# Channel relu on ScalarE and residual addition on GpSimd for three of four batches, in a recurrence-and-mixer kernel

## Chip, cores and metric

The kernel runs on one core of a Trainium2 chip. The metric is device time in microseconds for one execution. The time before is the median of 7 runs, 212.28 us (211.8 to 213.85). The engines are called by their usual names and the profile's: TensorE (PE; PEld is its weight load), VectorE (DVE), ScalarE (ACT), GpSimd (POOL) and SyncE (SP), whose queue issues most transfers.

## What is computed

The first half is a linear recurrence over 768 steps for 4 batches and 8 heads of 40 channels. The second half is a mixer on the result `x` (4 x 768 x 320):

```python
for t in range(S):                      # for every batch and head
    y[:, :, t] = einsum('bhd,bhde->bhe', rt, state)
    Sa = einsum('bhde,bhe->bhd', state, at)
    state = state * wt[:, :, None, :] - einsum('bhd,bhe->bhde', Sa, bt)
    state = state + einsum('bhd,bhe->bhde', vt, kt)
...
theta = x @ w_theta
zr, zi = x * cos(theta), x * sin(theta)
u = x + einsum('ts,bsd->btd', w_tok_r, zr) + einsum('ts,bsd->btd', w_tok_i, zi)
return u + maximum(u @ w_ch, 0.0)
```

The last line is the one that the change touches: the channel matmul `u @ w_ch`, its relu, and the residual addition of `u`.

## The kernel before, in words

The 768 steps of a batch are cut into 6 tiles of 128 steps; the 24 tiles of the 4 batches are worked one behind the other, all 8 heads at once.

For each tile, `prep` takes logarithms and cumulative sums of the decay (`lw`, `ex`, `sx`, `we`), scales the inputs on GpSimd (`kb` L696, `ah` L700, `v` L705) and transposes them on TensorE, ScalarE copying the results out of PSUM (L625). `scores` makes four 128x1024 blocks of step-by-step products on TensorE (L750, matmuls that use 64 rows of the array) and multiplies each by a mask on DVE (L755: `psi`, `phi`, `lamv`, `lamu`). `recurrence` solves the tile and carries the state to the next one: matmuls L783 and L789, copy `nx` on ScalarE (L795), matmuls L801, copy `nu` (L805), matmuls L822, then `sum` on DVE (L833) and the new state `gt` on GpSimd (L837). `readout` makes the tile's `x` (matmuls L885 to L894, then L901 on DVE), and `theta` multiplies it by `w_theta` (L910) and stores it through ScalarE (`th`, L920).

When a batch's tiles are done, `sines` takes sine and cosine on ScalarE (`cs`, L934, with another table of functions than the exponentials: a table load at L934 and one back at L1070), and GpSimd multiplies them by `x` into `zr` and `zi` (L946). Then `mix_row` makes each of the batch's 6 rows: 12 matmuls of 320 columns (L964), `u` on DVE (L974), a transpose of `u` (L865), the channel matmul (L910 with `wch`), the last step `oo` on DVE (L983) and the store (L986, on SP's queue). The rows of one batch run beside the tiles of the next; those of the last batch end the kernel.

The order of the work isn't the order of the code. Every instruction group is entered in a plan with an engine, a cost in nanoseconds, what it reads and writes, and a due time: `TIMES` by tile or row, plus `OFF` by kind, plus `ADJ` by the entry's number. A planner walks through modelled time, picks for each engine the entry with the least due time plus a penalty for waiting (`WAIT`) and for changing ScalarE's table (`TSWITCH`) or TensorE's 64- or 128-row form (`PSWITCH`), and deals out the 8 PSUM banks. What it yields is a fixed program: five queues, each worked in its order. Ahead of 14 us of planned time TensorE's gaps are filled with warm-up matmuls (L1064).

`u` has 4 buffers, `oo` has 3. What the change touches is the last step of `mix_row`:

```python
add("DVE", "oo", q, lambda: nc.vector.scalar_tensor_tensor(
    out=oo, in0=ps(ck)[:, 0:DM], scalar=0.0, in1=u[:, 0:DM], op0=ALU.max,
    op1=ALU.add), 488, [ck, ("u", q % 4)], [("oo", q % 3)], at="row")
add("SP", "st", q, lambda: nc.sync.dma_start(out=out_r[bi, j], in_=oo), 350,
    [("oo", q % 3)], [], at="row", work=550)
```

Of the kernel before, what the change touches and what calls it, by code (L numbers as in the profile page):

```python
# [11 lines left out]
AF = mybir.ActivationFunctionType  # L12
ALU = mybir.AluOpType
# [217 lines left out]
def tail(n):  # L231
# [4 lines left out]
    ah=-52.11, ch=49.75, cs=-52.92, ea=13.09, egd=-104.06, egt=-143.6, ekb=68.26, enu=18.9,  # L236
    enut=-16.67, er=39.64, eth=-122.81, eut=-51.5, ev=51.59, ew=15.76, ewt=-188.11, ex=-112.25,
    exp=-6.71, ext=81.47, gd=18.03, gt=35.48, kb=-27.06, la=-23.53, lb=-26.79, lk=-21.79,
    ln=-12.91, loadr=-13.5, lv=-12.45, lw=-26.87, mlu=184.93, mlv=69.19, mphi=153.16,
    mpsi=133.2, nu=29.59, nut=8.5, nx=-47.05, oo=28.87, r=113.01, row=16.53, sin=118.93,  # L240
    slu=-23.3, slv=25.75, sphi=-42.65, spsi=-87.98, st=17.74, ta=-28.45, th=19.17, tkb=15.03,
    tr=9.43, tv=-9.54, uadd=-2.7, ut=65.67, v=-4.95, wdma=168.22, wgt=-13.67, wi=-19.42,
    wt=-25.32, x0=-70.93, xt=30.93, y=-14.3, z=183.08)
WAIT, TSWITCH, PSWITCH = 1393.81, 654268.0, -24719.0
TIMES = dict(
    tile=[
        -86.14, -69.58, -37.21, -14.07, -14.8, 2.38, 2.2, 20.46, 24.1, 33.31, 50.51, 55.4,
        82.34, 92.68, 113.54, 132.24, 115.95, 137.46, 159.05, 157.81, 174.6, 187.04, 146.21,
        211.1],
    row=[  # L250
        69.81, 38.63, 41.84, 41.57, 7.21, -11.02, 134.23, 117.63, 149.79, 184.39, 169.21,
        207.36, 168.53, 187.12, 225.65, 155.58, 163.42, 84.66, 319.84, 314.41, 401.22, 514.77,
        559.98, 419.59],
    rel=[
        -33.63, 39.77, 64.32, 56.8, -226.72, 86.46, 80.14, -8.42])
ADJ = {
    0: -6.37, 1: 8.3, 2: -7.89, 3: -12.04, 4: -3.57, 5: 1.5, 6: 4.24, 7: 0.99, 8: 6.36,
    9: 16.34, 10: 5.24, 11: -0.26, 12: -20.38, 13: -2.84, 14: -4.42, 15: 1.56, 16: 1.04,
    17: 0.94, 18: -5.49, 19: 25.76, 20: -18.69, 21: 14.82, 22: -35.14, 23: 15.33, 24: 9.3,
    25: -0.9, 26: -5.18, 27: 5.69, 28: -20.76, 29: -7.52, 30: 16.91, 31: -9.14, 32: 26.44,  # L260
    33: -24.48, 34: 0.09, 35: -6.49, 36: -4.07, 37: 19.8, 38: -3.88, 39: 31.9, 40: -21.52,
    41: 27.32, 42: 5.23, 43: 3.89, 44: 2.28, 45: 6.35, 46: -3.55, 47: 4.36, 48: -0.72,
    49: 17.27, 50: 2.89, 51: 1.03, 52: -8.63, 53: 4.26, 54: -15.55, 55: -4.73, 56: -4,
    57: -2.18, 58: -36.01, 59: 3.02, 60: 4.49, 61: 28.68, 62: 0.32, 63: 2.69, 64: 4.61,
    65: 15.52, 66: 3.33, 67: 7.9, 68: 19.92, 69: -24.92, 70: -19.56, 71: 7.32, 72: 2.32,
    73: 21.16, 74: -8.51, 75: 1.62, 76: 1.58, 77: 12.52, 78: 2.22, 79: 1.98, 80: -8.26,
    81: 9.13, 82: 8.74, 83: -3.97, 84: 6.44, 85: 30.89, 86: 20.89, 87: 4.91, 88: -18.97,
    89: -1.02, 90: -39.76, 91: -5.91, 92: 11.36, 93: -22.13, 94: 15.62, 95: 10.71, 96: 3.64,
    97: 16.75, 98: -15.21, 99: -9.38, 100: 13.66, 101: 49.35, 102: 24.08, 103: -4.48,
    104: -8.09, 105: 38.54, 106: 3.08, 107: 28.48, 108: -9.04, 109: 14.05, 110: -12.9,  # L270
    111: -1.07, 112: -11.73, 113: 3.1, 114: -8.22, 115: -12.87, 116: 8.88, 117: -2.6,
    118: -0.69, 119: -6.56, 120: 18.35, 121: -0.64, 122: -22.22, 123: -4.96, 124: 15.3,
    125: 6.35, 126: -27.45, 127: 3.64, 128: 1.51, 129: -6.26, 130: -3.4, 131: -2.3, 132: -1.17,
    133: -13.37, 134: -1.7, 135: -0.01, 136: 16.69, 137: -7.08, 138: -0.5, 139: 18.08, 140: 4,
    141: -0.64, 142: 9.44, 143: -8.52, 144: -11.7, 145: -10.97, 146: 0.84, 147: 21.7, 148: -33,
    149: -4.17, 150: -2.19, 151: -0.74, 152: -4.13, 153: -2.44, 154: 0.36, 155: 21.02,
    156: 8.83, 157: -17.49, 158: -2.38, 159: 37.49, 160: 13.92, 161: 5.6, 162: 7.91,
    163: -2.34, 164: 28.5, 165: -7.61, 166: -16.91, 167: 4.86, 168: -4.3, 169: -16.93,
    170: -8.59, 171: -1.86, 172: -10.98, 173: -29.57, 174: 1.8, 175: 2.06, 176: -1.04,
    177: -55.47, 178: -2.04, 179: -13.59, 180: -0.73, 181: 3.9, 182: -0.75, 183: -1.04,  # L280
    184: 12.94, 185: 2.38, 186: -6.65, 187: 3.87, 188: 3.65, 189: -4.21, 190: 26.25, 191: 1.91,
    192: 0.59, 193: 11.95, 194: 22.42, 195: -5.3, 196: -18.83, 197: -8.08, 198: -3.49,
    199: -3.43, 200: -4.4, 201: -6.72, 202: 12.03, 203: -1.66, 204: -17.55, 205: -31.63,
    206: 15.51, 207: -10.93, 208: -17.43, 209: -4.4, 210: 7.83, 211: -4.44, 212: 13.12,
    213: -41.95, 214: -19.49, 215: 14.31, 216: 13.59, 217: 7.03, 218: 16.79, 219: -9.08,
    220: 4, 221: -6.77, 222: -7.57, 223: 21.01, 224: -7.74, 225: 12.36, 226: 10.83, 227: -6.61,
    228: 9.69, 229: 21.68, 230: 5.78, 231: 18.68, 232: 16.71, 233: -6.88, 234: -3.19,
    235: 13.7, 236: -11.83, 237: 1.49, 238: -4.5, 239: -1.11, 240: -0.98, 241: -29.01,
    242: -4.88, 243: -5.11, 244: 5.26, 245: -11.98, 246: 9.82, 247: 29.31, 248: 21.76,
    249: 14.42, 250: 4.41, 251: 56.91, 252: 9.47, 253: 9.53, 254: -11.2, 255: 37.04, 256: 5.9,  # L290
    257: -22.1, 258: -17.04, 259: -17.49, 260: -41.5, 261: -4.34, 262: -3.59, 263: -5.07,
    264: 30.34, 265: 21.1, 266: -20.31, 267: -2.53, 268: 20.04, 269: 24.18, 270: 48.62,
    271: -24.19, 272: 9.87, 273: -6.59, 274: -9.32, 275: -1.27, 276: -0.86, 277: 12.73,
    278: -26.81, 279: 8.18, 280: 28.16, 281: -38.2, 282: 0.14, 283: -1.42, 284: 8.61,
    285: -2.21, 286: -0.27, 287: -1.87, 288: -5.91, 289: 4.5, 290: -1.14, 291: 2.76,
    292: -3.89, 293: 15.58, 294: 0.21, 295: -2.51, 296: -19.83, 297: -21.12, 298: -13.52,
    299: 2.18, 300: -17.63, 301: -12.94, 302: 10.61, 303: -10.77, 304: 11.43, 305: -26.03,
    306: 14.21, 307: 28.47, 308: 11.2, 309: 5.66, 310: -14.04, 311: -10.82, 312: -16.59,
    313: 4.16, 314: -35.35, 315: 16.87, 316: 10.71, 317: -0.13, 318: -19.63, 319: -22.89,
    320: 27.35, 321: -9.39, 322: -2.42, 323: -2.29, 324: -1.41, 325: -19.26, 326: 16.71,  # L300
    327: -20.77, 328: -0.92, 329: -9.88, 330: -10.4, 331: -5.42, 332: -16.26, 333: 20.65,
    334: -7.61, 335: 0.88, 336: -2.65, 337: 25.72, 338: 30.25, 339: 7.19, 340: -17.23,
    341: -7.43, 342: 12.14, 343: -2.56, 344: -0.53, 345: 2.9, 346: -3.34, 347: 0.67,
    348: -0.46, 349: -15.55, 350: 29.58, 351: 12.01, 352: -0.77, 353: 7.51, 354: 22.83,
    355: 16.14, 356: 23.38, 357: -23.33, 358: -8.15, 359: 0.72, 360: -17.66, 361: 13.97,
    362: -12.12, 363: -15.15, 364: 30.36, 365: 36.88, 366: 6.29, 367: -27.99, 368: 9.94,
    369: -2, 370: -14.99, 371: -18.91, 372: 12.8, 373: 19.03, 374: 12.92, 375: -3.65,
    376: 5.67, 377: 19.41, 378: 16.41, 379: 17.22, 380: 0.63, 381: 13.8, 382: 20.91,
    383: 24.19, 384: 20.15, 385: -1.66, 386: -5.07, 387: -10.46, 388: -29.92, 389: 16.74,
    390: -9.91, 391: 16.93, 392: 1.46, 393: 20.84, 394: -5.9, 395: -0.31, 396: 2.31,  # L310
    397: -37.32, 398: -8.5, 399: -15.55, 400: 0.56, 401: 1.35, 402: 3.17, 403: -25.65,
    404: 11.11, 405: 11.05, 406: 2.98, 407: -3.53, 408: 15.93, 409: 4.06, 410: 7.86,
    411: -7.48, 412: 10.14, 413: 5.27, 414: -27.1, 415: 18.16, 416: 18.6, 417: -34.62, 418: 17,
    419: -22.51, 420: 42.85, 421: 20.44, 422: 33.09, 423: 3.62, 424: -7.25, 425: 7.78,
    426: 36.81, 427: -3.15, 428: -13.12, 429: -33.79, 430: -9.03, 431: 1.34, 432: -23.24,
    433: -17.08, 434: -6.39, 435: -1.15, 436: 8.79, 437: 14.46, 438: 30.49, 439: -4.36,
    440: -4.34, 441: 2.29, 442: 25.14, 443: 26.81, 444: -8.67, 445: -14.52, 446: 14.84,
    447: 27.71, 448: -14.26, 449: 6.26, 450: 12.09, 451: 16.34, 452: -8.66, 453: -1.78,
    454: 28.27, 455: -6.98, 456: -2.29, 457: 46.71, 458: -19.59, 459: -12.28, 460: 34.9,
    461: -2.98, 462: 3.94, 463: -23.98, 464: 3.42, 465: 30.57, 466: 1.45, 467: 5.05,  # L320
# [153 lines left out]
def kernel(  # L474
# [14 lines left out]
    nc = tc.nc  # L489
# [3 lines left out]
    DM = H * D  # L493
# [608 lines left out]
```

## Time and profile before

| what | us |
|---|---|
| median of 7 runs (lowest, highest) | 212.28 (211.8, 213.85) |
| the profiled execution | 212.28 |
| its span, first to last instruction | 210.5 |
| TensorE busy | 195.4 |
| DVE busy | 174.2 |
| ScalarE busy | 154.4 |
| GpSimd busy | 127.4 |
| mask multiplies L755, 96 of them | 116.6 |
| row matmuls L964, 288 of them | 81.3 |
| last steps L983, 24 of them | 11.3 |

TensorE ran at its full granted clock throughout. Matmuls overlap each other, so the sum of their durations is more than the time that TensorE needs for them: the 288 row matmuls take 0.30 us each, but start 0.136 us apart where nothing holds them up. Busy times of the other engines overlap a little as well: an instruction of 0.48 us on DVE is followed by the next one's start 0.40 us after its own.

A line of the profile's groups reads: line, engine, operation, output and input by the program's names, shapes, count, then busy time in us, mean ns of one, and idle time of the engine ahead of it with what ended it. A line of the stretches reads: from:to, length, busy us (instructions) of PE, PEld, DVE, ACT and POOL, granted clock, share of the DMA engines, GB/s. A line of the waits reads: who waited for whom, us in total, how many times, the longest.

### The profile page before, as it was taken

Reading aid. Unit: us, or ns where it says so; the run is one execution under the profiler, and the core shown is the slowest. Engines: PE = TensorE matmul, PEld = TensorE weight load, DVE = VectorE, ACT = ScalarE, POOL = GpSimd, SP = SyncE. Lnnn points to the kernel's source line nnn. Section 1 sums busy time; section 2 is a strip of 40 time slices with the busy share of each in tenths; the row PEclk is TensorE's granted clock in tenths of the full one; section 3 lists DMA queues with packets and bytes.
Section 4 is the critical chain, followed back from the end, with each engine's and each line's share of the span. In section 5 each row is a group of like instructions: output and inputs, shape, how many; then the busy total and the mean of one; then the engine's idle time right before and its main releaser. Section 6 shows DMA issues by size and latency. Waiting matters only on the chain.

```text
span 210.5 us, 8135 instructions
## 1 busy us (share of the span) xinstructions
PE 195.4 (93%) x3375; PEld 157.2 (75%) x3375; DVE 174.2 (83%) x277; ACT 154.4 (73%) x366; POOL 127.4 (61%) x186
## 2 busy tenths in 40 slices
PE   7777988788999999999999999999999999999993
PEld 7655876677878788887777888778887777887771
DVE  7399986799999987998788778989999987657533
ACT  2685878998799869945997967978799978371211
POOL 3206266779978987875098773786558964614000
PEclk9999999999999999999999999999999999999999
DMA  6999989989999998989989989999994010003122
GB/s 113 203 167 214 168 156 183 181 167 170 194 197 156 204 163 162 159 155 193 194 163 197 191 148 164 176 155 215 202 192 100 0 69 3 31 22 107 39 89 93
DMA packets 134181, 30.82 MB, mean 146 GB/s; under 512 B 125824, under 2 KB 134144, under 8 KB 134144
## 3 DMA queue, kind: packets, MB, share of 16 engines
q1 hardware_dynamic: 131712, 27.54, 67.1%
q0 software_dynamic: 2432, 2.77, 8.5%
q8 instruction: 26, 0.43, 0.8%
q14 instruction: 11, 0.09, 0.1%
HBM read 29.13 MB, written 3.93 MB: 157 GB/s over the span
## 4 chain that ended last, share of the span: by engine, by line
PE 58%; ACT 9%; DVE 5%; POOL 3%; issue 2%; POOLq 0%; ACTq 0%; DVEq 0%
PE ps_s L964 16%; PE ps_s L622 10%; PE ps_s L910 8%; PE ps_d L750 7%; PE ps_s L865 3%; ACT L934 2%; PE ps_s L801 2%; PE ps_s L894 2%; ACT cs L934 2%; PE ps_s L892 1%; PE ps_s L1012 1%; PE ps_s L789 1%; PE ps_s L885 1%; PE ps_s L733 1%; PE ps_s L783 1%
## 5 line engine op out<-in xcount | busy, mean ns | idle before, releaser
L696 POOL TENSOR_TENSOR kb<-raw_kb,ex 128x320 bf16<-128x320 f32 x44 | 37.7, 869 | 23.4 <-ACT vT L625 9.7
L964 PE MATMUL ps_s<-zr,wtok_r 128*128 128x320 bf16 x144 | 40.7, 299 | 0.0
L964 PE MATMUL ps_s<-zi,wtok_i 128*128 128x320 bf16 x144 | 40.6, 299 | 0.0
L755 DVE TENSOR_TENSOR psi<-ps_d,mask_p 128x1024 bf16<-128x1024 f32 x24 | 29.2, 1217 | 3.7 <-PE ps_d L750 3.7
L755 DVE TENSOR_TENSOR lamu<-ps_d,mask_p 128x1024 bf16<-128x1024 f32 x24 | 29.2, 1216 | 2.2 <-PE ps_d L750 2.1
L755 DVE TENSOR_TENSOR phi<-ps_d,mask_n 128x1024 bf16<-128x1024 f32 x24 | 29.1, 1214 | 1.3 <-PE ps_d L750 1.1
L755 DVE TENSOR_TENSOR lamv<-ps_d,mask_p 128x1024 bf16<-128x1024 f32 x24 | 29.1, 1213 | 0.4 <-PE ps_d L750 0.3
L946 POOL TENSOR_TENSOR zr<-cs,x 128x320 bf16<-128x320 f32 x23 | 17.9, 795 | 14.1 <-ACT cs L934 14.0
L700 POOL TENSOR_TENSOR ah<-raw_a,we 128x320 bf16<-128x320 f32 x22 | 19.0, 865 | 6.6 <-ACT we L689 3.5
L974 DVE TENSOR_TENSOR u<-ps_s,x 128x320 bf16<-128x320 f32 x24 | 11.6, 487 | 10.7 <-PE ps_s L964 10.7
L946 POOL TENSOR_TENSOR zi<-cs,x 128x320 bf16<-128x320 f32 x23 | 18.0, 797 | 1.3 <-ACT cs L934 1.3
L625 ACT COPY kbT<-ps_s 128x512 f32<-128x512 f32 x24 | 14.2, 592 | 5.7 <-PE ps_s L622 5.3
L750 PE MATMUL ps_d<-aT,kbT 64*128 64x128 bf16 x384 | 17.2, 218 | 0.9 <-ACT aT L625 0.4
L964 PEld LDWEIGHTS <-wtok_r 128*128 128x128 bf16 x144 | 14.1, 98 | 4.2
L625 ACT COPY uT<-ps_s 128x192 f32<-128x192 f32 x24 | 7.5, 320 | 12.8 <-PE ps_s L865 12.5
L964 PEld LDWEIGHTS <-wtok_i 128*128 128x128 bf16 x144 | 14.1, 98 | 3.8
L622 PE MATMUL ps_s<-ident,kb 128*128 128x128 bf16 x192 | 14.9, 219 | 1.1 <-POOL kb L696 0.6
L685 DVE TENSOR_TENSOR sx<-ps_s,lw 128x320 f32<-128x320 f32 x24 | 11.5, 483 | 5.1 <-ACT ex L682 5.1
L892 PE MATMUL ps_s<-kb,lamv 128*128 128x40 bf16 x192 | 15.3, 180 | 0.1
L894 PE MATMUL ps_s<-kb,lamu 128*128 128x40 bf16 x192 | 14.9, 179 | 0.4 <-DVE lamu L755 0.4
L983 DVE SCALAR_TENSOR_TENSOR oo<-ps_s,u 128x320 f32<-128x320 f32 x24 | 11.3, 484 | 4.4 <-PE ps_s L910 4.3
L750 PEld LDWEIGHTS <-kbT 64*128 64x128 bf16 x384 | 11.2, 94 | 4.8 <-issue 1.5
(119 smaller groups left out, 583.7 us busy)
## 6 DMA issues: line engine op xcount, KB each, us to landing
raw_a<-in_a_dram SPq DMA_DIRECT2D x24, 160.0 KB, 4.3
raw_kb<-in_b_dram SPq DMA_DIRECT2D x24, 160.0 KB, 3.9
raw_w<-in_w_dram SPq DMA_DIRECT2D x24, 160.0 KB, 4.2
raw_v<-in_v_dram SPq DMA_DIRECT2D x24, 160.0 KB, 4.2
raw_kb<-in_k_dram SPq DMA_DIRECT2D x24, 160.0 KB, 3.7
raw_r<-in_r_dram SPq DMA_DIRECT2D x24, 160.0 KB, 3.8
out_dram<-oo SPq DMA_DIRECT2D x24, 160.0 KB, 1.9
wrow_r<-in_moe_w_tok_r_dram POOLq DMA_DIRECT2D x6, 192.0 KB, 5.1
```

What stands on the lines that cost most here:

```text
L622: nc.tensor.transpose(out=dst[:, c:c + 128], in_=pair(src, g), identity=ident)
L625: nc.scalar.copy(out=out.bitcast(FP32), in_=in_)
L696: lambda j=j: (nc.vector if fast else nc.gpsimd).tensor_tensor(out=paired(kb[:, j])[:, :, :, 0:D], in0=natural(raw_kb[s4][:, j]), in1=invW ...
L700: lambda: (nc.vector if fast else nc.gpsimd).tensor_tensor(out=paired(ah)[:, :, :, 0:D], in0=natural(raw_a[i % 6]), in1=Wi, op=ALU.mult),
L750: nc.tensor.matmul(t[:, q, g, :], lhsT=lhs[rows(q), g * 128:(g + 1) * 128], rhs=rhs[rows(q), g * 128:(g + 1) * 128], start=True, stop=True)
L755: add("DVE", kindm, i, lambda: nc.vector.tensor_tensor(out=dst.rearrange("p a b c -> p (a b) c"), in0=ps(p).rearrange("p a (g c) -> p (a g ...
L892: nc.tensor.matmul(o, lhsT=lamv[:, p, g, :], rhs=kb[:, 0, h, 0:D], start=first, stop=False, skip_group_check=True)
L894: nc.tensor.matmul(o, lhsT=lamu[:, p, g, :], rhs=kb[:, 1, h, 0:D], start=False, stop=True, skip_group_check=True)
L910: nc.tensor.matmul(dst, lhsT=lhs[:, kt, :], rhs=rhs[:, kt, :], start=kt == 0, stop=kt == 2)
L946: nc.vector if fast else nc.gpsimd).tensor_tensor(
L964: nc.tensor.matmul(ps(pk)[:, 0:DM], lhsT=wtok[nm][:, s, j * 128:(j + 1) * 128], rhs=zs[c][:, s], start=n == 0 and c == 0, stop=n == NT - 1 ...
L974: add("DVE", "uadd", q, lambda: nc.vector.tensor_tensor(out=u[:, 0:DM], in0=ps(pk)[:, 0:DM], in1=x[:, 0:DM], op=ALU.add), 488, [pk, ("x", ...
```

## The change

For the rows of the first three batches (18 of 24) the last step is taken apart: ScalarE writes the relu of the channel matmul from PSUM into `oo`, and GpSimd adds `u` to `oo` in place. For the last batch's 6 rows it stays on DVE. All due times are other ones too, and the entries behind the first row have other numbers, since 18 entries are new; so the planner yields another order on every engine.

```diff
@@ OFF, WAIT, TSWITCH, PSWITCH, TIMES, ADJ: every value is another one
-    ... oo=28.87, r=113.01, row=16.53, ...
-WAIT, TSWITCH, PSWITCH = 1393.81, 654268.0, -24719.0
+    ... oo=-24.03, oop=0.1, r=86.08, relu=62.85, ...
+WAIT, TSWITCH, PSWITCH = 1802.17, 792912.0, -33791.0
@@ mix_row
         oo = oo_t[q % 3]
-        add("DVE", "oo", q, lambda: nc.vector.scalar_tensor_tensor(
-            out=oo, in0=ps(ck)[:, 0:DM], scalar=0.0, in1=u[:, 0:DM], op0=ALU.max,
-            op1=ALU.add), 488, [ck, ("u", q % 4)], [("oo", q % 3)], at="row")
+        if bi < B - 1:
+            add("ACT", "relu", q, lambda: nc.scalar.activation(
+                out=oo, in_=ps(ck)[:, 0:DM], func=AF.Relu), 432, [ck], [("oo", q % 3)], at="row")
+            add("POOL", "oop", q, lambda: nc.gpsimd.tensor_tensor(
+                out=oo, in0=oo, in1=u[:, 0:DM], op=ALU.add), 800,
+                [("oo", q % 3), ("u", q % 4)], [("oo", q % 3)], at="row")
+        else:
+            add("DVE", "oo", q, lambda: nc.vector.scalar_tensor_tensor(
+                out=oo, in0=ps(ck)[:, 0:DM], scalar=0.0, in1=u[:, 0:DM], op0=ALU.max,
+                op1=ALU.add), 488, [ck, ("u", q % 4)], [("oo", q % 3)], at="row")
         add("SP", "st", q, lambda: nc.sync.dma_start(out=out_r[bi, j], in_=oo), 350,
             [("oo", q % 3)], [], at="row", work=550)
```

The lines of `mix_row` behind this place stand some lines lower in the changed kernel: the relu is L987, the addition L989, the step left on DVE L993, the store L996; those ahead of it are 3 lines lower (L755 becomes L758).

## The prediction, made before the result was known

> **What bounds the kernel now.** I read the busy table first, then the chain, then the stretches, then the spacing of TensorE's starts.
>
> ```profile
> span 210.5 us, 8135 instructions
> PE 195.4 (93%) x3375; PEld 157.2 (75%) x3375; DVE 174.2 (83%) x277; ACT 154.4 (73%) x366; POOL 127.4 (61%) x186
> ...
> PE 58%; ACT 9%; DVE 5%; POOL 3%; issue 2%; POOLq 0%; ACTq 0%; DVEq 0%
> ```
>
> PE fills the span and most of the chain, but its busy time counts overlapped matmuls. The busy times by stretch (PE, PEld, DVE, ACT, POOL) say where it is short of work:
>
> ```profile
> 15.00:30.00 15.00, 13.41 (x266) 10.82 (x265) 14.87 (x20) 11.02 (x30) 7.20 (x9) 1.00 1.00 186
> ...
> 45.00:60.00 15.00, 13.68 (x290) 11.32 (x287) 14.47 (x17) 13.20 (x38) 13.94 (x20) 1.00 1.01 175
> 60.00:70.00 10.00, 9.31 (x194) 7.58 (x191) 10.00 (x14) 9.77 (x20) 8.47 (x14) 1.00 1.04 187
> 70.00:131.00 61.00, 60.30 (x1039) 49.02 (x1034) 51.84 (x74) 47.37 (x114) 43.00 (x61) 1.00 0.94 172
> 131.00:170.00 39.00, 38.44 (x755) 31.49 (x755) 37.33 (x49) 34.60 (x83) 29.51 (x42) 1.00 0.73 143
> 170.00:207.20 37.20, 37.07 (x449) 27.42 (x443) 23.56 (x41) 16.86 (x40) 10.66 (x15) 1.00 0.15 53
> ```
>
> Up to 70 us DVE is full and PE is not; from 70 us on, where the first mixing row starts, PE is full. To see how full, I add up issue time from start-to-start spacings in the PE timeline:
>
> ```profile
> 130.29 0.21 PE L789 MATMUL ps_s<-v,psi 128*128 128x40 bf16 x2
> 130.43 0.40 PE L750 MATMUL ps_d<-aT,kbT 64*128 64x128 bf16 x8
> 130.76 0.58 PE L910 MATMUL ps_s<-wch,uT 128*128 128x320 bf16 x3
> 131.18 0.30 PE L964 MATMUL ps_s<-zr,wtok_r 128*128 128x320 bf16 x1
> ```
>
> A 320-column matmul takes 0.136 us of PE, one of 128 columns 0.0555, of 80 columns 0.0355, of 40 or fewer 0.025, a warm-up one 0.107. Eight score matmuls (L750, 64 rows) take 0.225, and each run of them costs 0.19 more for going into and out of the 64-row form (0.11 us instead of 0.025 ahead of the run above, 0.148 behind its last matmul instead of 0.053). With the counts of the groups: 459 x 0.136 + 872 x 0.0555 + 320 x 0.0355 + 888 x 0.025 + 68 x 0.107 + 96 x 0.225 + 67 runs x 0.19 = 186.5 us within rounding. The last matmul ends at 207.2 us, so PE stands idle for 20.7 us. Ahead of the first row matmul (70.1 us) the sum is 55.2: 14.9 us idle. Behind it, 131.3 of 137.1: **only 5.8 us idle, over two thirds of the kernel**. By the semaphore that each of these late gaps waited for, about 1.5 us are DVE's, 0.4 DVE's or ScalarE's, 2.2 ScalarE's. The 3.3 us behind the last matmul (last addition, store, end) stay.
>
> **The change, part by part.** The profiled run took 212.28 us, which is also the median; 1.8 us of it lie outside the span. I sum against it.
>
> *Removed:* 18 of the 24 instructions of L983 on DVE. Each takes 0.48 us busy and moves the next start by 0.40:
>
> ```profile
> 90.41 0.48 DVE L983 SCALAR_TENSOR_TENSOR oo<-ps_s,u 128x320 f32<-128x320 f32 x1
> 90.81 1.21 DVE L755 TENSOR_TENSOR lamv<-ps_d,mask_p 128x1024 bf16<-128x1024 f32 x1
> ```
>
> That is 8.7 us of busy time, 7.2 us of DVE's queue, all behind 78 us, where PE and not DVE is full.
>
> *Added:* 18 ScalarE relus and 18 GpSimd additions. A relu on 128x320 from PSUM isn't in the trace; the nearest rows are the plain copy and the slower exp of nearly the same shape:
>
> ```profile
> L920 ACT COPY th<-ps_s 128x320 f32<-128x320 f32 x23 | 9.8, 427 | 2.7 <-PE ps_s L910 2.4
> L682 ACT ACTIVATE ex<-ps_s 128x328 f32<-128x328 f32 x24 | 10.6, 447 | 3.0 <-PE ps_s L678 2.9
> L946 POOL TENSOR_TENSOR zr<-cs,x 128x320 bf16<-128x320 f32 x23 | 17.9, 795 | 14.1 <-ACT cs L934 14.0
> L696 POOL TENSOR_TENSOR kb<-raw_kb,ex 128x320 bf16<-128x320 f32 x44 | 37.7, 869 | 23.4 <-ACT vT L625 9.7
> ```
>
> I take 0.43 us for a relu (bounds 0.427 and 0.447) and 0.80 for an addition, which is contiguous as zr is (bounds 0.795 and 0.869). Together 7.7 us on ScalarE and 14.4 us on GpSimd, which are 73% and 61% busy. Between 131 and 170 us, where three relus go, ScalarE has 4.4 us free and needs 1.3. Hidden as work; not as a wait (second rival).
>
> The Trainium skill speaks against both halves. "ScalarE: Activation LUTs", section "Rules for kernel authors", wants relu and add on VectorE, which it calls up to about three times faster; the rows here say 0.427 us for a copy out of PSUM on ScalarE against 0.484 for L983 on DVE. By the rule 18 relus would be up to 26 us of ScalarE, an estimate, instead of 7.7. "GPSIMD Engine Reference", section "4.1 Engine selection", calls GpSimd about half as fast for two inputs; L946 agrees in kind, 0.795 us on GpSimd against 0.493 on DVE for the last tile.
>
> *A longer hand-over:* PSUM to output was one instruction, and is now relu, semaphore, addition, some 0.75 us more (0.43 + 0.80 - 0.48). A store waits so much longer in SP's queue with loads of the next tiles behind it; ten of the 18 have loads behind them. The loads run tiles ahead, and behind 60 us no engine waits for a load by more than 1.1 us, so I cost this at nothing; without that cover it is 0.75 us a store.
>
> *Moved:* all due times changed, so every queue has a new order. Its instruction lists show three things. ScalarE loads 11 tables in place of 13 (L934 and L1070, 1.283 us each): 2.6 us back. PE has the same work less two warm-ups, but 74 runs of scores in place of 67: +1.33 - 0.21 = **+1.1 us of PE**, 187.6 in all. And the first row stands earlier: ahead of its first `u` (L974) DVE has 36 mask multiplies (spacing 1.13) in place of 38, 10 `sx` in place of 12, 7 `x` in place of 8: 58.5 us of queue in place of 62.0. PE has 53.9 ahead of the first row matmul in place of 55.2.
>
> **The sum.** Up to the first row DVE sets the pace (10.00 of 10.00 us busy just before it), so that row should come up to 3.5 us sooner. PE's work ahead of it falls by only 1.3, so 2.2 us of PE's 14.9 us of idle time go; none go if ScalarE's sines or the loads pace that stage. I take 2.2, as the DVE column is nearest to full. Behind the first row DVE is relieved and PE can get back at most the 1.9 us that DVE shares in; I take 1.0, since half of such gaps are latency of one step and not a queue (bounds 0 and 1.9). The relus cost ScalarE's queue something: bounds 0 and 1.7 (DVE waited 1.7 us for this very matmul between 60 and 195 us); I take 0.5. Sum: 212.28 + 1.1 - 2.2 - 1.0 + 0.5 = **210.7 us**. The bounds make 209.3 with everything good (212.28 + 1.1 - 2.2 - 1.9), and lower if rows pulled forward also fill other early gaps: 14.9 us lie there, and I allow 1 us, 208.3.
>
> **The rivals.**
> - *DVE's free time stays DVE's.* PE is the bound behind 70 us, and the front is paced by the sines: GpSimd's zr waits 14.0 us for `cs` in 4 waits. Then only +1.1 and -1.0 remain: 212.3 us. For it: 5.8 us idle in 137. Against: the full DVE column.
> - *Slower: ScalarE's queue becomes the wait.* A relu waits for its channel matmul as L983 did, but in a queue with the recurrence behind it: of the 18 relus two have `nx` and one each `nu` and `gd` within two places, and two of GpSimd's additions have a new state (L837) so close behind.
>
> ```profile
> DVE oo L983 <- PE ps_s L910: 4.3, 5, 1.2
> POOL gt L837 <- DVE sum L833: 7.1, 7, 3.7
> ```
>
>   Five waits in 24 of 0.86 us are 3.2 in 18; with two states held up for 0.75 each, 4.7 us at most. If the 1.7 us that fall between 60 and 195 us reach PE and nothing is won, the time is 212.28 + 1.1 + 1.7 = 215.1. It decides from about 1 us of net loss, 213.3, on: I give it 214.2. For it: PE's late gaps are ScalarE's more than DVE's (2.2 against 1.5), so work moves onto the engine that PE waits for. Against: ScalarE is 78% busy between 70 and 131 us, DVE 85%.
> - *Nothing changes in kind:* that L983 still runs for these rows is excluded by the lists: 6 are left on DVE.
>
> **How the numbers follow.** Forecast of 210.7 (208.3 to 211.2): 0.42. Unchanged within 0.5%, which is about what a measurement can tell from no change (211.2 to 213.3): 0.28. Slower (213.3 to some 216): 0.30. Leaving out about a tenth at each end gives 208.3 to 214.8.
>
> **What would show it.** Right: the first row matmul starts 1 to 3.5 us before 70.1; PE's idle time ahead of it falls from 14.9 to about 12.7; DVE is some 8.7 us less busy; relus near 0.43 us, additions near 0.80; from there on PE at 96% or more. Wrong: the first row no earlier (first rival); waits of ScalarE for L910 ahead of relus above 2 us, longer waits of GpSimd ahead of L837 (now L840) and late PE idle time above 6 us (second rival).

## The result, and the profile after

The changed kernel takes 213.27 us (median of 24 runs, 212.05 to 214.59) against 212.20 us (61 runs) of the kernel before. The ratio is **1.0044** (95% interval 1.0029 to 1.0060): slower by 0.93 us by the ratio (1.07 us between the medians). That is clear of no change by the interval, and under 0.5%. The forecast was 210.7 us; the result lies in the case of "unchanged within 0.5%", which had a chance of 0.28. The profiled execution took 213.0 us, 0.7 more than the one of before.

The page of the changed kernel, its span, busy times and chain:

```profile
span 211.2 us, 8126 instructions
...
PE 195.5 (93%) x3373; PEld 157.1 (74%) x3373; DVE 167.3 (79%) x259; ACT 158.2 (75%) x382; POOL 141.1 (67%) x204
...
PE 64%; ACT 14%; DVE 10%; DMA 4%; issue 3%; SPq 1%; POOL 1%; ACTq 0%; DVEq 0%
```

DVE is 6.9 us less busy, GpSimd 13.7 us and ScalarE 3.8 us more: the work moved as written, and the span grew all the same. PE has the same busy time within 0.1 us. The chain now goes through ScalarE for 14% (9% before), DVE for 10% (5%) and transfers for 4%.

The stretches of the changed kernel (PE, PEld, DVE, ACT, POOL busy, then clock, DMA share, GB/s):

```profile
45.00:60.00 15.00, 14.62 (x309) 12.13 (x304) 14.81 (x18) 13.15 (x38) 12.71 (x19) 1.00 0.97 173
60.00:70.00 10.00, 9.58 (x178) 7.59 (x176) 9.86 (x13) 9.64 (x19) 9.31 (x15) 1.00 1.07 184
70.00:131.00 61.00, 60.40 (x1038) 48.82 (x1036) 49.11 (x68) 49.04 (x118) 49.21 (x69) 1.00 0.95 175
131.00:170.00 39.00, 38.03 (x768) 31.29 (x766) 37.19 (x46) 36.19 (x90) 30.76 (x44) 1.00 0.76 149
170.00:208.00 38.00, 37.03 (x441) 27.61 (x440) 20.39 (x33) 16.82 (x44) 16.99 (x23) 1.00 0.14 50
```

Up to 70 us PE is fuller than before (14.62 instead of 13.68 in 45 to 60 us): the front is better. From 70 to 170 us DVE has lost 2.9 us of work and PE has gained nothing from it.

The groups of the new step:

```profile
L989 POOL TENSOR_TENSOR oo<-oo,u 128x320 f32<-128x320 f32 x18 | 14.4, 798 | 13.9 <-ACT oo L987 13.7 <-DMA raw_v<-in_v_dram 0.2
...
L987 ACT ACTIVATE oo<-ps_s 128x320 f32<-128x320 f32 x18 | 7.9, 437 | 5.7 <-DMA out_dram<-oo 3.0 <-PE ps_s L913 2.0 <-POOL zr L949 0.6
```

An addition takes 0.798 us and a relu 0.437 us, as priced. But a relu waited 3.0 us for a transfer, the store that still held its output buffer.

**Where the 0.7 us went.** I add up PE's issue time for both kernels by the spacings of the prediction (done by program on each start, which puts the sums of before at 15.1 and 6.2 us of idle time instead of 14.9 and 5.8):

| us | before | after | difference |
|---|---|---|---|
| PE issue, whole kernel | 185.8 | 186.9 | +1.1 |
| first row matmul starts | 70.1 | 67.5 | -2.6 |
| PE idle ahead of it | 15.1 | 13.8 | -1.3 |
| PE idle behind it | 6.2 | 7.2 | +1.0 |
| last matmul ends | 207.2 | 207.9 | +0.7 |

The +1.0 is nearly one gap. It shows in the timeline of the changed kernel (start, duration, and in brackets what the engine waited for):

```profile
198.04 0.30 PE L967 MATMUL ps_s<-zi,wtok_i 128*128 128x320 bf16 x1
...
198.59 0.44 ACT L987 ACTIVATE oo<-ps_s 128x320 f32<-128x320 f32 x1 [3.02 <-DMA out_dram<-oo]
...
199.08 0.30 PE L967 MATMUL ps_s<-zr,wtok_r 128*128 128x320 bf16 x1 [0.74 <-ACT oo L987]
```

PE starts matmuls 1.04 us apart instead of 0.136: a gap of 0.90 us. The relu holds the PSUM bank that PE wants next, and the relu itself stands 3.02 us for the landing of an earlier store from the same output buffer. That store did not wait in SP's queue: it was issued at 194.78 us, 0.03 us after its addition ended. It took 3.71 us to land, against 2.5 in the median of this kernel's 24 stores. Of the 16 updates that report a landing, fifteen had come by 196.66 us and the last at 198.49. Had the last come with them, the relu would have ended at about 197.2 us (196.66 + 0.10 + 0.44, an estimate), ahead of the 198.18 at which PE wanted the bank.

One trace could be chance, but two other kernels of almost the same order with three buffers (e15 and e6 below) show the gap at the same place. Their relus stood 2.8 and 2.4 us and started 0.1 us after a landing that took 3.5 and 3.1 us; PE lost 0.65 and 0.28 us. In e15's timeline the view names a matmul that ended at about the same time:

```profile
197.69 0.44 ACT L987 ACTIVATE oo<-ps_s 128x320 f32<-128x320 f32 x1 [2.77 <-PE ps_s L967]
```

### The profile page after: what moved, and what is told of

It is laid out like the page before. It is cut to its first block, busy times and chain, and to the rows that moved or that the text cites. A ratio compares the mean times of both kernels' runs of the same rounds, so it can differ in the third digit from the quotient of the medians.

```text
span 211.2 us, 8126 instructions
## 1 busy us (share of the span) xinstructions
PE 195.5 (93%) x3373; PEld 157.1 (74%) x3373; DVE 167.3 (79%) x259; ACT 158.2 (75%) x382; POOL 141.1 (67%) x204
## 4 chain that ended last, share of the span: by engine, by line
PE 64%; ACT 14%; DVE 10%; DMA 4%; issue 3%; SPq 1%; POOL 1%; ACTq 0%; DVEq 0%
PE ps_s L967 16%; PE ps_s L625 11%; PE ps_d L753 10%; PE ps_s L913 7%; PE ps_s L868 3%; DMA raw_kb<-in_k_dram 2%; DVE lamu L758 2%; PE ps_s L897 2%; ACT cs L937 2%; PE ps_s L825 2%; PE ps_s L804 2%; PE ps_s L1022 2%; DMA out_dram<-oo 2%; DVE psi L758 2%; ACT rT L740 2%
## 5 line engine op out<-in xcount | busy, mean ns | idle before, releaser
L758 DVE TENSOR_TENSOR psi<-ps_d,mask_p 128x1024 bf16<-128x1024 f32 x24 | 29.2, 1218 | 6.8 <-PE ps_d L753 6.7
L758 DVE TENSOR_TENSOR lamu<-ps_d,mask_p 128x1024 bf16<-128x1024 f32 x24 | 29.2, 1217 | 1.3 <-PE ps_d L753 1.2
L758 DVE TENSOR_TENSOR lamv<-ps_d,mask_p 128x1024 bf16<-128x1024 f32 x24 | 29.1, 1215 | 1.1 <-PE ps_d L753 1.0
L758 DVE TENSOR_TENSOR phi<-ps_d,mask_n 128x1024 bf16<-128x1024 f32 x24 | 29.1, 1214 | 0.2
L989 POOL TENSOR_TENSOR oo<-oo,u 128x320 f32<-128x320 f32 x18 | 14.4, 798 | 13.9 <-ACT oo L987 13.7
L977 DVE TENSOR_TENSOR u<-ps_s,x 128x320 bf16<-128x320 f32 x24 | 11.6, 487 | 14.8 <-PE ps_s L967 10.2
L895 PE MATMUL ps_s<-kb,lamv 128*128 128x40 bf16 x192 | 15.4, 180 | 0.0
L904 DVE TENSOR_TENSOR x<-ps_s,we 128x320 bf16<-128x320 f32 x24 | 11.6, 485 | 4.7 <-PE ps_s L897 3.9
L897 PE MATMUL ps_s<-kb,lamu 128*128 128x40 bf16 x192 | 14.9, 180 | 0.5 <-DVE lamu L758 0.3
L625 PE MATMUL ps_s<-ident,kb 128*128 128x128 bf16 x192 | 14.7, 219 | 0.7 <-DVE kb L699 0.3
```

The source lines that it names most:

```text
L625: nc.tensor.transpose(out=dst[:, c:c + 128], in_=pair(src, g), identity=ident)
L758: add("DVE", kindm, i, lambda: nc.vector.tensor_tensor(out=dst.rearrange("p a b c -> p (a b) c"), in0=ps(p).rearrange("p a (g c) -> p (a g ...
L895: nc.tensor.matmul(o, lhsT=lamv[:, p, g, :], rhs=kb[:, 0, h, 0:D], start=first, stop=False, skip_group_check=True)
L897: nc.tensor.matmul(o, lhsT=lamu[:, p, g, :], rhs=kb[:, 1, h, 0:D], start=False, stop=True, skip_group_check=True)
L989: add("POOL", "oop", q, lambda: nc.gpsimd.tensor_tensor(out=oo, in0=oo, in1=u[:, 0:DM], op=ALU.add), 800, [("oo", q % 3), ("u", q % 4)], [ ...
```

## The experiments

Ratios are to runs of the kernel before on the same chip, with 95% intervals. The first table gives the measured ones together; "runs" are runs of score matmuls, idle times are PE's, ahead of the first row matmul and behind it, by the accounting above, from one profiled execution each.

| kernel | runs | PE issue | idle ahead | idle behind | ratio |
|---|---|---|---|---|---|
| before | 67 | 185.8 | 15.1 | 6.2 | 1 |
| after | 74 | 186.9 | 13.8 | 7.2 | 1.0044 (1.0029, 1.0060) |
| e1 after's order, step on DVE | 74 | 186.9 | 14.9 | 10.1 | 1.0146 (1.0095, 1.0196) |
| e2 before's order, step split | 67 | 185.8 | 15.2 | 14.7 | 1.0362 (1.0322, 1.0403) |
| e3 before without 18 last steps | 67 | 185.8 | 14.8 | 6.3 | 1.0018 (0.9989, 1.0047) |
| e4 before, 20 more runs | 87 | 189.6 | 15.4 | 6.5 | 1.0146 (1.0110, 1.0183) |
| e5 after, 6 output buffers | 74 | 186.9 | 15.1 | 6.1 | 1.0016 (0.9992, 1.0041) |
| e6 after, 9 runs fewer | 65 | 185.2 | 17.9 | 7.0 | 1.0135 (1.0105, 1.0165) |
| e7 before, 4 runs fewer | 63 | 185.1 | 15.8 | 7.2 | 1.0040 (1.0018, 1.0063) |
| e8 e6 with 6 buffers | 65 | 185.2 | 18.7 | 6.6 | 1.0086 (1.0056, 1.0116) |
| e9 before's order, relu alone | 67 | 185.8 | 15.2 | 12.7 | 1.0317 (1.0289, 1.0345) |
| e10 e2, additions later | 67 | 185.8 | 16.7 | 13.5 | 1.0432 (1.0398, 1.0465) |
| e11 e5, 4 late runs fewer | 70 | 186.2 | 15.2 | 10.5 | 1.0184 (1.0154, 1.0213) |
| e12 before, 3 late runs fewer | 64 | 185.2 | 15.4 | 10.2 | 1.0168 (1.0138, 1.0199) |
| e13 before, replanned (484) | 67 | 185.8 | 15.0 | 10.7 | 1.0209 (1.0168, 1.0249) |
| e14 before, replanned (496) | 70 | 186.4 | 15.2 | 9.6 | 1.0193 (1.0132, 1.0255) |
| e16 before, replanned (510) | 69 | 186.2 | 15.6 | 11.1 | 1.0255 (1.0179, 1.0331) |
| e15 after, replanned (relu 450) | 74 | 186.9 | 13.4 | 6.7 | 1.0041 (1.0016, 1.0067) |
| e17 after, replanned (addition 820) | 74 | 186.9 | 13.7 | 8.9 | 1.0115 (1.0081, 1.0149) |
| e18 after, replanned (relu 500) | 74 | 186.9 | 15.1 | 11.0 | 1.0204 (1.0123, 1.0285) |

Read the columns downward: PE's work differs by 4.5 us at most, and by under 2 us outside e4. What separates a good time from a bad one is the idle time behind the first row: 6.1 to 7.2 us in the kernels up to 1.0044, 8.9 to 14.7 us in those above 1.01, but for e4, which has more work, and e6, whose idle time lies ahead. (In e1, e5, e6, e8, e11, e17 and e18 the granted clock dipped in one to three slices of the first 45 us, which adds up to 1.3 us to their idle time ahead, as e5 beside the changed kernel shows; their idle time behind isn't touched.)

The clock doesn't explain the result, though it differs. Its mean was below 0.995 in 21 of the changed kernel's 25 executions and in 10 of the 77 of before that were measured beside e1 to e18. But the four executions of the changed kernel at 0.998 or more took 212.96 to 213.27 us, all above the median of before.

### e1 and e2: the split and the order, each without the other

e1 keeps the order of after and gives the step back to DVE; e2 keeps the order of before and splits the step.

```diff
@@ e1, in after's mix_row
-            add("ACT", "relu", q, lambda: nc.scalar.activation(
-                out=oo, in_=ps(ck)[:, 0:DM], func=AF.Relu), 432, ...
-            add("POOL", "oop", q, lambda: nc.gpsimd.tensor_tensor(
-                out=oo, in0=oo, in1=u[:, 0:DM], op=ALU.add), 800, ...
+            add("ACT", "relu", q, lambda: nc.vector.scalar_tensor_tensor(
+                out=oo, in0=ps(ck)[:, 0:DM], scalar=0.0, in1=u[:, 0:DM], op0=ALU.max,
+                op1=ALU.add), 432, ...
+            add("POOL", "oop", q, lambda: None, 800, ...
@@ e2, in before's entry "oo", for bi < B - 1
-    nc.vector.scalar_tensor_tensor(out=oo, in0=ps(ck), scalar=0.0, in1=u, ...)
+    nc.scalar.activation(out=oo, in_=ps(ck), func=AF.Relu)
+    nc.gpsimd.tensor_tensor(out=oo, in0=oo, in1=u, op=ALU.add)
```

> The changed kernel's order with the last step of the 18 rows back on DVE as one instruction, at the place of the relu; nothing else. PE theory (from 70 us on TensorE's issue time is the bound, and what the change lost is 7 more runs of score matmuls, 1.3 us, in the new order): the split itself is worth about nothing, 212.6 to 213.4 us. Queue rival (the split costs because relus and additions stand in queues that TensorE waits for): 212.2 or less. DVE rival (relief of DVE is worth much and the new order only hides it): 215 or more, since DVE gets 7.2 us back.

> The order of before with relu on ScalarE and addition on GpSimd for the 18 rows, at the place of the old last step. PE theory: 211.9 to 212.8 us, no difference that counts. Queue rival: 213.2 or more. DVE rival: 211 or less.

e1 took 216.47 us, e2 220.99, against 213.21. Neither half does any good alone: the order of after without the split is 1% slower than with it, the split in the order of before costs 7.8 us. By their times e1 is what the DVE rival forecast (215 or more) and e2 what the queue rival did (213.2 or more); the PE theory missed both. In e1 the late gaps of PE that waited for DVE alone are 4.7 us instead of 1.3, and 2.0 us of PE's waits name the step itself:

```profile
PE ps_s L625 <- DVE oo L987: 0.9, 2, 0.6
```

So in the order of after, 18 steps put on DVE do cost. That isn't the same as a gain from taking them off, which e3 tests. GpSimd's waits in e2, and PE's longest behind 70 us:

```profile
POOL oo L986 <- ACT oo L985: 13.3, 12, 5.7
...
PE ps_s L622 <- POOL ah L700: 2.0, 3, 1.0
```

12 of its 18 additions stood for the relu, 13.3 us in all, up to 5.7, with all that lies behind them in the queue, such as the inputs `ah` that PE waits for. I took that for the cause; e9 and e10 test it.

### e3: DVE relieved, and nothing else

```diff
@@ in before's entry "oo", for bi < B - 1
-    nc.vector.scalar_tensor_tensor(out=oo, in0=ps(ck), scalar=0.0, in1=u, ...)
+    pass
```

> The order of before; the last step of the 18 rows is left out altogether (the stores write zeros, so relu and residual addition of three batches are missing). It is the most that relief of DVE can be worth in this order. PE theory: 211.2 to 212.2 us, since DVE shares in only 1.9 us of TensorE's idle time behind 70 us. DVE rival: 209 or less of 212.2, most of the 7.2 us.

e3 leaves out the relu and the residual addition of three batches (three memsets fill the buffers at the start, so that the stores have something to write). 213.80 us against 213.21, ratio 1.0018 with 1 inside its interval. Its busy times:

```profile
PE 194.8 (93%) x3375; PEld 156.2 (74%) x3375; DVE 167.1 (79%) x259; ACT 154.6 (74%) x366; POOL 128.1 (61%) x189
```

DVE is as light as in the changed kernel (167.1 us), neither of the other engines carries anything in return, and PE's late idle time is 6.3 us as it was (6.2), with 1.5 us of it by DVE's semaphore in both. **Relief of DVE behind 70 us is worth nothing** in this order, not the 1.0 us of the prediction.

### e4: the price of a run of score matmuls

```diff
+    # behind 70 us: where two groups of scores stand side by side and a group of
+    # 128-row matmuls follows that depends on neither, it is moved between them
+    if a.start > FROM and a.mode == 64 and b.mode == 64 and c.mode == 128:
+        move_up(c, b)
```

> The order of before, in which behind 70 us 20 pairs of score groups that stood side by side are parted by the 128-row matmul group that followed them (87 runs of scores in place of 67); same work. PE theory: each run costs 0.19 us of TensorE that nothing hides: plus 3.8, 215.5 to 216.3 us. DVE rival: masks set the pace, half or more is hidden: 214.2 or less. Queue rival has no view.

Ratio 1.0146, 3.5 us between the medians for 20 runs: 0.17 us each, near the 0.19 of the spacings. PE's issue sum is what the kernel pays from 70 us on, and the +1.1 us of the prediction stands.

### e5: more output buffers in the changed kernel

```diff
-    oo_t = sb("oo", [128, DM], FP32, 3)
+    oo_t = sb("oo", [128, DM], FP32, 6)
...
-        oo = oo_t[q % 3]
+        oo = oo_t[q % 6]
```

> The changed kernel, same order, with six buffers for the last step's result in place of three. In the changed kernel one relu waits 3.0 us for an earlier store to land, and TensorE stands still for 0.9 us behind it (at 198 us). Theory (TensorE's issue time is the bound; new loss is 1.1 us of issue time for 7 more runs plus 0.9 us of this wait): 0.9 us less than the changed kernel, so 212.3 where before is 212.2, ratio to before about 1.000 in place of 1.0044. Queue rival (the loss is spread over ScalarE's and GpSimd's queues): no change, ratio 1.0035 to 1.005.

Ratio 1.0016 instead of 1.0044, but the intervals touch. The trace is clearer than the time. ScalarE's waits ahead of relus are now

```profile
ACT oo L987 <- PE ps_s L913: 2.4, 5, 0.8
```

and nothing else: the 3.0 us for the store are gone, the gap of 0.90 us at 198 us is gone, and the late idle time is 6.1 us, 1.1 less. So in these two executions the extra idle time of the changed kernel is the output buffer's. The ratio is nearer to the theory's 1.000 than to the queue rival's 1.0035 to 1.005, but its interval reaches into the latter. The time doesn't fall below that of before.

### e6, e7, e8, e11, e12: fewer runs of score matmuls

If an extra run costs 0.19 us, taking runs away should pay. A group of scores is moved next to its neighbour where little lies between:

```diff
+    # a lone group of scores a, and b, the next one, less than GAP away:
+    if m < len(pe) and m > k + 1 and t < GAP:
+        move_down(a, b) or move_up(b, pe[k + 1])
```

e6 and e8 (with six buffers) join 9 runs in the order of after, e7 joins 4 in that of before, GAP 0.7 us; e11 (with six buffers, GAP 1.5) and e12 (GAP 3.0) only behind the first row.

> The changed kernel with 9 of its 74 runs of score matmuls joined to a neighbouring run (a score group is put behind, or ahead of, the few 128-row matmuls that stood between the two): 65 runs, same work. Theory: 9 x 0.19 = 1.7 us less of TensorE's time, less what the delayed masks cost: ratio to before 0.996 to 0.999. Queue rival: TensorE's order isn't the loss; ratio 1.003 or more.

> The kernel before, treated as in the last experiment; only 4 of 67 runs can be joined. Theory: 0.76 us less, ratio 0.9955 to 0.999. If joining costs more in masks that come late than it saves: above 1.000.

> Both mends of the changed kernel together: 65 runs and six buffers. Theory: 1.7 + 0.9 us less than the changed kernel, 210.6 where before is 212.2, ratio 0.991 to 0.995: faster than both. Queue rival: 1.002 or more.

> The changed kernel with six output buffers and, only behind the first mixing row, four runs of score matmuls fewer (70 instead of 74, none touched ahead of 70 us). Theory (joining lost before because it made masks late ahead of the first row, where VectorE sets the pace; behind it TensorE is full): 4 x 0.19 = 0.8 us less than with six buffers alone, ratio 0.996 to 1.000. Rival (a joined pair delays what waits for the moved group wherever it is): as with six buffers alone or above, 1.0016 to 1.008.

> The kernel before with three runs of score matmuls fewer, all behind the first mixing row (64 instead of 67). Theory: 3 x 0.19 = 0.6 us less, ratio 0.995 to 0.999. Rival (joining delays what waits for the moved group by more than it saves): 1.000 to 1.008.

The theory missed in all five, on the slow side; the rivals of e6, e7 and e8 were right, and e11 and e12 are slower than their rivals allowed, too. The issue sum fell as expected (186.9 to 185.2 in e6), and the idle time rose by more: by 4.1 us ahead of the first row in e6 (2.8 beside e5), where 7 of its 9 joins lie, by 4.0 us behind it in e12 and 4.4 in e11 (beside e5). My second theory, that joins lose only where DVE sets the pace, fell with e11 and e12. A moved group of scores makes its mask multiply late there as well: PE's late waits by DVE's semaphores rose from 1.5 to 4.2 us in e12, and those by DVE's, or by DVE's and ScalarE's together, from 1.9 (e5) to 5.0 us in e11. e8 beside e6 (1.0086 against 1.0135, intervals that touch) points to a gain from six buffers a second time, 0.6 us in the medians, 0.4 us in the late idle time.

### e9 and e10: which half of the split costs in the order of before

e9 moves the relu alone, the addition stays on DVE. e10 is e2, with each addition and its store put behind the next work of GpSimd that is planned at least 3 us later.

```diff
@@ e9, for bi < B - 1
+    nc.scalar.activation(out=oo, in_=ps(ck), func=AF.Relu)
+    nc.vector.tensor_tensor(out=oo, in0=oo, in1=u, op=ALU.add)
@@ e10, for bi < B - 1
+    nc.scalar.activation(out=oo, in_=ps(ck), func=AF.Relu)
+    late[q] = (oo, u, out_r[bi, j])
...
+        for n in sorted(late):
+            if (("oo", n % 3) in o.writes or ("u", n % 4) in o.writes
+                    or (o.eng == "POOL" and o.start > begun[n] + DELAY)):
+                finish(n)
```

> In the order of before, the relu of the first three batches is ScalarE's and the addition stays on VectorE. Theory (what cost 7.7 us when both halves were moved in this order is GpSimd's queue, in which the state products stood behind additions that waited for a relu): most of that is gone, 212.5 to 214.5 us, ratio 1.000 to 1.008, and GpSimd's waits are as in before. Rival (the relu itself costs it, as ScalarE's queue stands while its channel matmul is late): 1.02 to 1.036 again, with long waits of ScalarE for L910.

> As the split in the order of before, but each addition of GpSimd (and its store) is put behind the next work of GpSimd that is planned at least 3 us later, so that the relu is done when the addition's turn comes. Theory (it is the place in GpSimd's queue that costs): the waits of GpSimd's additions for ScalarE fall from 13.3 us to below 5 and the ratio from 1.036 to 1.000 to 1.012. Rival (the relu in ScalarE's queue costs it): the ratio stays above 1.025.

e9 took 219.43 us, e10 221.70, against 212.60. **GpSimd's queue isn't needed for the cost:** with no addition on GpSimd it is still 6.8 us, and with the additions later it is 9.1, although their waits for ScalarE fell from 13.3 to 1.3 us as the theory of e10 wanted. In e2 itself PE did wait for GpSimd; without those waits others took their place. e10 brings one of its own, since its later stores hold the buffers longer, and PE waits 1.5 us behind this relu:

```profile
ACT oo L985 <- DMA out_dram<-oo: 3.6, 1, 3.6
```

The groups of e9:

```profile
L985 ACT ACTIVATE oo<-ps_s 128x320 f32<-128x320 f32 x18 | 7.8, 438 | 2.1 <-PE ps_s L910 2.1
...
L986 DVE TENSOR_TENSOR oo<-oo,u 128x320 f32<-128x320 f32 x18 | 11.7, 656 | 8.9 <-ACT oo L985 8.9
```

The ratio is the rival's, its reason isn't: ScalarE waited only 2.1 us for L910. What e2, e9 and e10 share is 18 relus, 7.8 us, in a queue of ScalarE that was planned without them, and a second half that waits for them (8.9 us of DVE here). Which of the two carries the 6.8 us, these runs don't separate.

### e13 to e18: the same work in other orders

Every alteration of an order had cost something, with the split or without. So the last six let the planner itself make new orders of unchanged work. The only edit is the cost that it assumes for the last step:

```diff
@@ e13, e14, e16: before, entry "oo"
-            op1=ALU.add), 488, ...
+            op1=ALU.add), 484, ...        (496, 510)
@@ e15, e17, e18: after, entries "relu" and "oop"
-    relu 432, oop 800
+    relu 450, oop 800      (432 and 820; 500 and 800)
```

> The kernel before, with the planner's cost of the last step at 484 ns (the measured mean) in place of 488: the same work in a slightly different order, 67 runs of score matmuls as before. Theory (the place in the order is what decides, and the order of before is a lucky one): 1.003 to 1.015. Rival (the split itself costs the 0.44%, an order made by the planner is as good as another): 0.998 to 1.003.

> As e13 with 496 ns: 70 runs of score matmuls in place of 67, a larger change of the order. Theory: 1.005 to 1.02. Rival: 0.998 to 1.004 (three more runs are 0.6 us).

> As e13 with 510 ns: 69 runs of score matmuls. Theory (the order decides): 1.005 to 1.02. Rival (any order of the planner is as good): 0.998 to 1.003.

> The changed kernel, with the planner's cost of the relu at 450 ns in place of 432: the same work in another order, 74 runs. Theory (the split itself is worth about nothing, its order is a draw from the same scatter): 1.003 to 1.02, no higher as a family than e13, e14 and e16. Rival (the split costs by itself): above the reorderings of before by 0.4% or more.

> The changed kernel, with the planner's cost of the addition at 820 ns in place of 800: 74 runs, the smallest change of its order. Theory (the order decides): 1.002 to 1.02, in the same scatter as the reorderings of before. Rival (the split costs by itself): above those by 0.4% or more.

> As e15 with 500 ns for the relu: 74 runs, a large change of the order. Theory (the order decides): 1.003 to 1.02, in the same scatter as the reorderings of before. Rival (the split costs by itself): above those by 0.4% or more.

The kernel before, replanned: 1.0209, 1.0193, 1.0255. The changed kernel: 1.0044, and replanned 1.0041, 1.0115, 1.0204. The theory's sense holds, its sizes were too small for e13 and e16, and just so for e18. e13 is the cleanest case, since its instructions are those of before and so is its PE issue sum, 67 runs included. Its busy times, and PE's longest waits behind 70 us:

```profile
PE 196.2 (91%) x3375; PEld 156.2 (73%) x3375; DVE 175.1 (82%) x277; ACT 154.8 (72%) x366; POOL 127.1 (59%) x186
```

```profile
PE ps_s L894 <- DVE lamu L755: 1.2, 1, 1.2
PE ps_s L1012 <- DMA wrow_r<-in_moe_w_tok_r_dram: 0.7, 1, 0.7
PE ps_s L865 <- DVE x L901: 0.7, 1, 0.7
```

**Four nanoseconds in the planner's cost of one step are worth 4.3 us**, over four times what the whole change is. The busy times are those of before within 1 us; three single waits, for a mask multiply, a transfer of weights and an output tile, none of which stands behind 70 us in the order of before (PE's longest wait there is 0.3 us), make 2.6 us of it. All of it lies in the idle time behind the first row, 10.7 us instead of 6.2. At the other end stands e15: its profiled execution (212.08 us) is the shortest profiled one of the changed family, its median of 10 runs is 213.21.

So nothing here says that the split costs by itself: the rival wanted the changed family 0.4% above that of before, and its three replanned orders (mean 1.012) stand below the three of before (mean 1.022). With three draws each and such a scatter this is no proof of a gain either. The result compares two orders, each from due times of its own, and no order that was run has a lower median ratio than that of before, though e3 and e5 can't be told from it.

## Why the prediction was wrong, point by point

- **PE's sum, +1.1.** Right: 185.8 to 186.9 us, and e4 shows that an extra run is paid (0.17 us). The products of the prediction add up to 186.0, not 186.5, so the idle times of before are 15.1 and 6.2 us in place of 14.9 and 5.8; the difference stays.
- **The front, -2.2.** Right in mechanism, 0.9 us too large: -1.3. The first `u` came 3.5 us sooner (73.2 to 69.7), exactly as DVE's queue said, but the first row matmul that PE starts with came 2.6 sooner, and 1.3 of that was less work ahead of it. The first `u` isn't the first row matmul; the step took the advance of the one for that of the other.
- **DVE's relief, -1.0.** **This is the step that failed in kind.** e3 takes the same 7.2 us off DVE and gains nothing (late idle time 6.2 to 6.3), and in the changed kernel the gaps that waited for DVE went from 1.5 to 1.3 us. The prediction took half of those gaps for DVE's queue; by e3 nothing of them came back when the queue got shorter. e3 shows it in the order of before; in the order of after only the reverse was run, and there the steps put back on DVE cost 2.9 us of idle time (e1). The first rival had this right in its words, "DVE's free time stays DVE's", but its sum kept the -1.0 (and comes to 212.4, not 212.3), and it denied the front, which did come.
- **The relus, +0.5, and the longer hand-over, at nothing.** The relus' own waits for their matmul were 2.0 us, and those gaps of PE that waited for ScalarE alone went only from 2.2 to 2.4 us, 0.9 of them new. The cost came where I had put zero: the hand-over is longer, the store lands late, the relu behind it waits 3.0 us for the buffer and PE 0.90. I looked for a load behind the store in SP's queue and not for the next relu behind its buffer. How much of this is the longer hand-over and how much the late last part of the landing isn't separated; half of the 3.71 us was that last part.
- **By its own terms** the sum was +1.1 - 2.2 - 1.0 + 0.5; measured is +1.1 - 1.3 and +1.0 for the two last together, of which 0.9 is the buffer's. That is, within rounding, the 0.7 us between the two profiled executions, where the forecast had -1.6: 0.9 us of the miss are the front's and 1.5 the late idle time's.
- **The second rival's signs.** Late idle time above 6 us: yes, 7.2. ScalarE's waits for L910 above 2 us: just reached. Longer waits of GpSimd ahead of the new state: no, 1.4 us instead of 7.1. Its mechanism did not act in the changed kernel, probably because that order had been made with the relus in it. Its price, 1.7 us, is far below what the relus and what waited for them cost in an order that was not (6.8 us, e9).
- **What would show it:** relus near 0.43 and additions near 0.80 us held. (The factor of three that the prediction takes from the Trainium skill, "ScalarE: Activation LUTs", section "Rules for kernel authors", is given there for bf16 with a single source. Here the relu reads f32 from PSUM: 0.437 us, against 0.484 for DVE's relu and addition in one.) "DVE 8.7 us less busy" did not, it is 6.9, close to the 7.2 of queue (18 x 0.40), since each step overlaps the next. "PE at 96% or more" from the first row on did not: (186.9 - 53.7) of 140.4 us is 95%.
- **The deeper fault** is the basis of the sum. It took the late idle time of before, 5.8 us, as a stock from which a lighter engine could only take. It belongs to one order; the planner deals it anew with every change, and the kernels run here have 6.1 to 14.7 us. From a kernel that stands at the low end, "all due times changed" should have cost some expected idle time and a long upper tail: the medians of the six replanned ones lie 0.9 to 5.2 us above the runs of before beside them.

What stays open: which of ScalarE's lateness and the second half's wait carries the cost of e9; and whether other due times would bring the split kernel below the kernel before. Six buffers brought it to within 0.2% and a changed cost to within 0.4%, none below, and the two were not tried together.

## What to carry to other kernels

When an order made by a planner keeps the bounding engine 95% full, don't count on its remaining gaps: here work taken from another engine filled none of them. Price such a change by what it does to the bounding engine's own work and to buffers that are held longer. Before you credit or blame an edit, replan the old kernel with one to a few per cent on one cost: here that alone moved it by 1.9 to 2.6%, and a smaller effect can't be told from that of the order it came with. And when one step becomes two on different engines, follow the output buffer to its next writer, not only the store's queue.

## What the hardware showed that was not expected

An addition on DVE with both operands in SBUF (L986 in e9) isn't a fixed 0.48 us like the steps that read PSUM. The timeline of e9:

```profile
95.18 0.49 DVE L986 TENSOR_TENSOR oo<-oo,u 128x320 f32<-128x320 f32 x1 [0.79 <-ACT oo L985]
...
111.52 1.69 POOL L696 TENSOR_TENSOR kb<-raw_kb,ex 128x320 bf16<-128x320 f32 x2
...
112.53 1.02 DVE L986 TENSOR_TENSOR oo<-oo,u 128x320 f32<-128x320 f32 x1 [0.46 <-ACT oo L985]
113.17 1.10 POOL L700 TENSOR_TENSOR ah<-raw_a,we 128x320 bf16<-128x320 f32 x1
113.48 0.48 DVE L901 TENSOR_TENSOR x<-ps_s,we 128x320 bf16<-128x320 f32 x1
```

The seven additions during which GpSimd computed nothing took 0.47 to 0.49 us; the other eleven took 0.52 to 1.02, 0.76 in the mean, while L901, which reads PSUM beside the same GpSimd instruction, kept its 0.48. GpSimd's own instruction (`ah`, L700) took 1.10 us, where its mean in the kernel before is 0.87. The Trainium skill, "GPSIMD Engine Reference", section "1. Specifications", says that GpSimd shares its SBUF interfaces with VectorE, with contention when the latter reads two inputs from SBUF; these rows agree. It makes (0.656 - 0.484) x 18 = 3.1 us of DVE's busy time in e9. So the residual addition behind a relu on ScalarE is cheap on neither engine: on GpSimd it takes 0.80 us, on DVE 0.66.
